# Polysketch attention and a sigmoid-gated FFN in one kernel: a denominator's sum moved forward on ScalarE, a product batch moved ahead of the Gram sums, and one PSUM bank exchanged

## The chip, the core and the metric

The kernel runs on one core of a Trainium2 chip. The metric is the device time of an execution in microseconds (us). It was 308.38 us in the median of six runs of the kernel before (308.05 to 309.17).

The engines have short names in the profile: PE is TensorE (matrix products), PEld is its loading of weights, DVE is VectorE, ACT is ScalarE, POOL is GpSimd, SP is SyncE, which here only issues DMAs. Each engine works through its own list of instructions in the order in which the program gives them. Between engines semaphores make one wait for another.

## What is computed

```python
# q, k, v: (4, 4, 1088, 32) = batch, heads, tokens, head_dim; S1, S2: (8, 32)
def phi(x):
    a = einsum('rd,bhsd->bhsr', S1, x)
    b = einsum('rd,bhsd->bhsr', S2, x)
    return einsum('bhsi,bhsj->bhsij', a, b).reshape(..., 64)
q_p, k_p = phi(q), phi(k)
kv  = einsum('bhsf,bhsd->bhfd', k_p, v)
z   = sum(k_p, axis=2)
num = einsum('bhsf,bhfd->bhsd', q_p, kv)
den = einsum('bhsf,bhf->bhs', q_p, z)[..., None] + 1e-06
x   = (num / den), laid out as (4352, 128) = (batch * tokens, heads * head_dim)
# w_gate, w_val: (128, 1536), w_out: (1536, 128)
out = (1 / (1 + exp(-(x @ w_gate))) * (x @ w_val)) @ w_out
```

The three weights and S1, S2 arrive as 64-bit numbers and are narrowed to 32 bits on the chip.

## The kernel before

**The FFN.** The 4352 tokens are cut into chunks of 512 (`tok_chk`), the 1536 hidden columns into 12 blocks of 128. `w1` makes a *wave*: for one chunk and one block, the gate and value products (L350) into a PSUM tile `wave`, and the sigmoid of the first on ScalarE (`sg`, L358). `glu` multiplies the two on VectorE (`g`, L371). `w2` multiplies by the block of w_out and adds up over the blocks in PSUM (`moeout`, L307), two waves behind. `slot(group, n)` emits a group of attention work and then n waves, so most of the attention of batches 1 to 3 lies between waves. In the first chunk the first wave is split into halves of 256 columns. The tokens of that chunk come from batch 0, so batch 0's first half of q must go through the attention before any wave can begin. That stretch, from the start to the first waves, is called the head here. All the edits lie in it.

**Order.** The program puts PE, DVE, ACT and POOL under a schedule written by hand (`tc.manual_schedule`): the order of calls in the code is the order of instructions on these four engines. Waits between engines, and waits for a tile's buffer to come free, are put in by the framework from what each instruction reads and writes.

**The head's attention, in the order of the code.** `turn_k` and `turn_q` transpose k and q in 32x32 blocks. `kps(0)` multiplies k by the sketches into PSUM tile `two`, and VectorE transposes that into `kab` (two instructions, L448). `ab((0, 0, 0))` and `ab((0, 1, 0))` make the a-products of q for the two pairs of heads (PSUM `wave`; ScalarE copies them to `asb`). `gram()` makes 36 small products of kab with itself (L460), from which z is formed; its PSUM tile is in bank `acc1`. ScalarE copies the result (`gs`), GpSimd masks it (`gh`). `spread_z` multiplies again (L487). `mask_z` puts the result into `zb` on VectorE (L498, L510). `ab(None, ...)` makes the b-products of q: those of pair 0 in tile `two`, those of pair 1 in a `wave` tile. It returns `mult00` or `mult10`, which multiply a and b on VectorE into `qp` (L567). `outer` (L520) forms the features of k, first for blocks 0 to 4, later for 5 to 8, and `kv0` (L628) adds their products with v up in `kvz`, bank `acc0`.

**`dn` and `divide`.** `dn(b, n, mid)` makes the denominators `dps` (L720; for batch 0's first half in bank `acc1`), then calls `mid`, then makes the numerators `nps` (L733). For the head `mid` is `rest`: the remaining `outer` and `kv0`, `kvd` (ScalarE copies kvz, L664), `ndt` (TensorE transposes the copy into bank `acc0`, L698, and ScalarE copies that to `nd`, L711). `dn` returns `divide`. This transposes dps (`dT`), adds 1e-6 (`rc`), takes the reciprocal (L752), spreads it with a transposition (`rb`, L756) and multiplies (`xT`, L767). In the head the sum with 1e-6 is on ScalarE (`sum_on_act`). In all other calls it is on VectorE (L751). `warm` gives TensorE a product that nobody reads.

**Narrowing.** `narrow` is a generator in four steps: step 0 clamps the high words on GpSimd (`cap`, L97) and scales the low words on ScalarE (`tail`, L101). Step 1 shifts and joins bits on VectorE (`head`, L105 and L109). Step 2 squares cap on ScalarE (`square`, L117, in a PSUM bank) and adds head and tail on GpSimd (L118). Step 3 combines the square and the sum on VectorE into `w_sb` (L121). `narrow_01(part, step)` does the first two columns' weights in three parts: part 0 is gate and value of column 0, part 1 those of column 1, part 2 the w_out of both. `narrow_w(j, step)` does column j, and `w1` calls it for columns 2 and up between the waves of the first chunk. The squares lie in PSUM banks `acc0` and `acc1`, each with one buffer, which the sums `moeout` use too. A new tile in a bank waits until the last reader of the tile before is through.

The weights' DMAs (`load_w`, six groups of three) are issued on SP from the start, after k, the sketches, the first half of q, and v.

Of the kernel before, what the change touches and what calls it, by code (L numbers as in the profile page):

```python
# [8 lines left out]
F32 = mybir.dt.float32  # L9
# [4 lines left out]
ACTF = mybir.ActivationFunctionType  # L14
MUL = ALU.mult

P = 128
# [3 lines left out]
def kernel(  # L21
# [12 lines left out]
    nc = tc.nc  # L34
# [19 lines left out]
    sbA = ctx.enter_context(tc.tile_pool(name="sbA", bufs=2))  # L54
# [124 lines left out]
    def narrow_01(part, step):  # L179
        if wide:  # L180
            if step == 0:
                i = (slice(0, 2), part) if part < 2 else (2, slice(0, 2))
                narrowing["01", part] = narrow(
                    w_sb[:, i[0], i[1]],
                    w_in[0][:, i[0], i[1]],
                    nc.gpsimd,
                    "acc0" if part == 1 else "acc1",
                )
            next(narrowing["01", part])

# [54 lines left out]
    def warm(*cols):  # L245
        t = psm.tile([P, 2, 512], F32, tag="wave", name="warm")
        one = [bass.AP(tensor=ones.tensor, offset=ones.offset, ap=[list(ones.ap[0]), [0, n]]) for n in cols]
        x = bass.AP(tensor=ones.tensor, offset=ones.offset, ap=[list(ones.ap[0]), [0, P]])
        for r in one:
            n = r.shape[-1]  # L250
            nc.tensor.matmul(out=t[:, 0, :n], lhsT=x, rhs=r, start=True, stop=True)  # L251
# [18 lines left out]
    for c in range(2):  # L270
        rows = slice(64 * c, 64 * c + 64)
        nc.vector.tensor_reduce(
            out=m_col[rows, c],
            in_=ident[rows].rearrange("p (k j) -> p j k", j=R),
# [3 lines left out]
    for t, x in ((e_row, id_h.rearrange("p h x -> p x h")), (e_head, id_h)):  # L278
        nc.vector.tensor_reduce(out=t, in_=x, axis=mybir.AxisListType.X, op=ALU.add)
    nc.vector.tensor_copy(  # L280
        out=e_sum,
# [6 lines left out]
    eps = const.tile([P, 1], F32, tag="eps")  # L288
    nc.gpsimd.memset(eps, 1e-6)
    zb = []  # L290
    for n in range(2):
        t = const.tile([P, H, 32], F32, tag=f"zb{n}", name=f"zb{n}")
# [239 lines left out]
    def ab(a_of=None, b_of=None, pool_b=None):  # L532

        mm = []
        if a_of is not None:
            aps = psm.tile([P, 2, 512], F32, tag="wave", name="aps")
            mm.append((a_of, aps, sa))
        if b_of is not None:
            pool, tag = (ps2, "two") if pool_b is None else pool_b
            bps = pool.tile([P, 2, 512], F32, tag=tag, name="bps")  # L540
            mm.append((b_of, bps, sb))
        for c in range(2):
            for m in range(2):
                for (bb, pr, n), dst, sx in mm:
                    h = 2 * pr + m
                    rows = slice(32 * h, 32 * h + 32)
                    t0, tn = q_chk[n]
                    nc.tensor.matmul(
                        out=dst[64 * c : 64 * c + 64, m, : 32 * tn],
                        lhsT=sx[rows, :],  # L550
                        rhs=qT_of[bb][rows, t0 : t0 + tn, c, :],
                        start=True,
                        stop=True,
                    )
        if a_of is not None:
            w = 32 * q_chk[a_of[2]][1]
            ASB[a_of] = sbA.tile([P, 2, 256], F32, tag="asb", name="asb", bufs=2)
            nc.scalar.copy(out=ASB[a_of][:, :, :w], in_=aps[:, :, :w])
        if b_of is not None:

            def mult():
                bb, pr, n = b_of
                if bb not in QP:
                    QP[bb] = sbA.tile([P, 2 * H * W1], F32, tag="qp", name="qp")
                t0, tn = q_chk[n]
                w = 32 * tn
                nc.vector.tensor_tensor(  # L567
                    out=half(QP[bb], n).rearrange("p (m c) w -> p c m w", m=2)[:, pr],
                    in0=bps[:, :, :w],
                    in1=ASB[b_of][:, :, :w],  # L570
                    op=MUL,
                )

            return mult
# [47 lines left out]
    def kv0(j_list):  # L622
        if 0 not in KVZ:
            KVZ[0] = pso.tile([P, TCH], F32, tag="acc0", name="kvz")
        for j in j_list:
            kr = 64 if j == 0 else P
            for h in range(H):
                nc.tensor.matmul(  # L628
                    out=KVZ[0][32 * h : 32 * h + 32, :F],
                    lhsT=v_t[0][:kr, h, j, :],  # L630
                    rhs=KP[0][:kr, h // 2, j, h % 2, :],
                    start=(j == 1),
                    stop=(j == NJK - 1),
                    skip_group_check=True,
                )
# [24 lines left out]
    def kvd(b):  # L660
        KVD[b] = sbA.tile([P, 2, 2, F], F32, tag="kvd", name="kvd")
        k0 = KVZ[b][:, : 2 * F]
        n = 2 if b > 0 else 1
        nc.scalar.copy(  # L664
            out=KVD[b][:, :n],
            in_=bass.AP(
                tensor=k0.tensor, offset=k0.offset, ap=[list(k0.ap[0]), [F, n], [0, 2], [1, F]]
            ),
        )
# [44 lines left out]
    def dn(b, n, mid=None):  # L714
        t0, tn = q_chk[n]
        w = 32 * tn
        bank = (moe["sum"] + 1) % 2 if moe["sum"] >= 0 else 1
        dps = pso.tile([P, TCH], F32, tag=f"acc{bank}", name="dps")
        for h in range(H):
            nc.tensor.matmul(  # L720
                out=dps[32 * h : 32 * h + 32, :w],
                lhsT=zb[b % 2][:, h, :],
                rhs=half(QP[b], n)[:, 2 * (h % 2) + h // 2, :],
                start=True,
                stop=True,
            )
        if mid is not None:
            mid()
        t = ps2.tile([P, 2, 512], F32, tag="two", name="nps")
        for h in range(H):  # L730
            for c in range(2):
                rows = slice(64 * c, 64 * c + 64)
                nc.tensor.matmul(  # L733
                    out=t[32 * h : 32 * h + 32, c, :w],
                    lhsT=ND[b][rows, 32 * h : 32 * h + 32],
                    rhs=half(QP[b], n)[rows, 2 * (h % 2) + h // 2, :],
                    start=True,
                    stop=True,
                )

        def divide(*parts, between=None, sum_on_act=None):
            dT = sbA.tile([P, 9, 32], F32, tag="dT", name="dT")
            nc.vector.transpose(out=dT[:, :tn].rearrange("p t c -> p (t c)"), in_=dps[:, :w])
            rc = sbA.tile([P, 9, 2], F32, tag="rc", name="rc")
            if sum_on_act is not None:
                nc.scalar.activation(
                    out=rc[:, :tn], in_=dT[:, :tn, :2], func=ACTF.Identity, bias=eps
                )
                sum_on_act()
            else:  # L750
                nc.vector.tensor_scalar_add(rc[:, :tn], dT[:, :tn, :2], 1e-6)  # L751
            nc.vector.reciprocal(out=rc[:, :tn], in_=rc[:, :tn])  # L752
            rb = sbA.tile([P, 9, 2, 32], F32, tag="rb", name="rb")
            for u0, u1 in parts or [(0, tn)]:
                r0 = rc[:, u0:u1]
                nc.vector.transpose(  # L756
                    out=rb[:, u0:u1].rearrange("p t c s -> p (t c s)"),
                    in_=bass.AP(
                        tensor=r0.tensor,
                        offset=r0.offset,  # L760
                        ap=[list(r0.ap[0]), [1, 2 * (u1 - u0)], [0, 32]],
                    ),
                )
                if between is not None and u0 == 0:
                    between()
                o = b * S + 64 * (t0 + u0)
                nc.vector.tensor_tensor(  # L767
                    out=xT[:, o : o + 64 * (u1 - u0)].rearrange("p (t c s) -> p c t s", c=2, s=32),
                    in0=t[:, :, 32 * u0 : 32 * u1].rearrange("p c (t s) -> p c t s", s=32),
                    in1=rb[:, u0:u1].rearrange("p t c s -> p c t s"),  # L770
                    op=MUL,
                )
            moe["ready"] = b * S + 64 * (t0 + tn)

        return divide

    steps = narrow(sr, sr_in, nc.vector) if wide else iter(())
    for _ in range(3):
# [9 lines left out]
        out=sk,  # L788
# [21 lines left out]
    kps(0)  # L810
    ab((0, 0, 0))
    ab((0, 1, 0))
    spread_z, mask_z = gram()
    mult00 = ab(None, (0, 0, 0))
    mult10 = ab(None, (0, 1, 0), (psm, "wave"))
    for part in range(3):
        narrow_01(part, 0)
# [6 lines left out]
    mask_z()  # L824


    def rest():
        for pi in range(2):
            outer(0, pi, 5, NJK)
        kv0(range(5, NJK))  # L830
        kvd(0)
        ndt(0)

    divide = dn(0, 0, rest)
    warm(512)

    def head0():
        narrow_01(0, 1)
        narrow_01(0, 2)

    def head1():
        narrow_01(1, 1)
# [2 lines left out]
        narrow_w(2, 0)  # L845
        narrow_w(3, 0)

    divide((0, 4), (4, 8), between=head1, sum_on_act=head0)
    narrow_01(1, 3)
    narrow_01(2, 1)  # L850
    narrow_01(2, 2)
# [85 lines left out]
```

## Time and profile before

One execution was profiled. It took 309.17 us, the highest of the six. Its span, from the first to the last instruction, is 307.3 us; 1.87 us lie around it.

| what | value |
|---|---|
| median of six runs | 308.38 us (308.05 to 309.17) |
| profiled execution: time, span | 309.17 us, 307.3 us |
| TensorE's granted clock | 1.000 |
| PE busy, 0 to 7.40 us | 4.71 us |
| PE busy, 7.40 to 23.50 us | 13.24 us of 16.10 |
| PE busy, 23.50 to 303.40 us | 279.65 us of 279.90 |
| DMA, 7.40 to 23.50 us | 341 GB/s |
| DVE, ACT, POOL busy, 7.40 to 23.50 us | 13.86, 7.34, 7.15 us |

A row of the timeline gives the start, the busy time, the engine, the line of the code, the operation, the tile written and those read, the shape, and a count: neighbouring instructions of one kind are put together. The bracket at its end is the time for which the engine sat idle before it, and what ended the wait. Where a wait is for several things, the bracket names the one that the profile saw last, which need not be the one that mattered. Rows of one engine can overlap by about 0.1 us[...]. The waits view adds up who waited for whom. The chain of waits goes back from the last instruction, each time to what released it.

### The profile page before, as it was taken

How to read it: one execution, taken by the hardware profiler on the slowest of the kernel's cores; microseconds unless marked ns; L12 is line 12 of the kernel's file. 1: busy time of each engine (PE TensorE's matmuls, PEld its weight loads, DVE VectorE, ACT ScalarE, POOL GpSimd, SP SyncE). 2: the span in 40 equal slices, each digit the busy share in tenths (PEclk: the TensorE clock that was granted, in tenths of full speed). 3: DMA queues.
4: the chain of work that ended last, by engine and by line, in shares of the span. 5: the costliest groups of instructions: out<-in, count | busy, mean ns of one | idle time of the engine just before them, and what ended most of it. 6: DMA issues, size and time to landing. Idle time of an engine off the chain costs nothing.

```text
span 307.3 us, 3606 instructions
## 1 busy us (share of the span) xinstructions
PE 297.6 (97%) x1361; PEld 136.4 (44%) x1361; DVE 155.0 (50%) x268; ACT 80.4 (26%) x150; POOL 34.8 (11%) x63
## 2 busy tenths in 40 slices
PE   6889999999999999999999999999999999999994
PEld 2433434444344444543444444444444444444683
DVE  4978789752836544463565542645232223222331
ACT  3355542322122222222123222212222222222220
POOL 2165541230000320000002300000000000000000
PEclk9999999999999999999999999999999999999999
DMA  7991422399602292242003920200001000200011
GB/s 205 360 335 45 122 63 114 80 174 169 185 0 34 71 221 56 60 104 96 0 0 87 235 61 2 35 0 2 0 10 24 0 0 5 31 0 0 6 29 17
DMA packets 29842, 23.35 MB, mean 76 GB/s; under 512 B 21185, under 2 KB 24769, under 8 KB 29825
## 3 DMA queue, kind: packets, MB, share of 16 engines
q1 hardware_dynamic: 25456, 15.28, 18.7%
q0 software_dynamic: 3456, 7.09, 11.6%
q10 hardware_dynamic: 912, 0.77, 1.0%
q8 instruction: 10, 0.16, 0.2%
q14 instruction: 8, 0.06, 0.1%
HBM read 19.86 MB, written 3.26 MB: 75 GB/s over the span
## 4 chain that ended last, share of the span: by engine, by line
PE 84%; DMA 10%; DVE 2%; POOL 1%; SPq 1%; issue 0%; ACT 0%; DVEq 0%; POOLq 0%
PE wave L350 52%; PE moeout L307 27%; DMA bq<-dq 4%; DMA w_in<-in_moe_w_val_dram 2%; DMA w_in<-in_moe_w_gate_dram 2%; DMA v<-in_v_dram 1%; PE nps L733 1%; PE dps L720 1%; PE kvz L642 1%; DMA out_dram<-o_sb 1%; PE cqps L587 1%; PE kps L438 1%; POOL qp L611 1%; POOL bq L611 0%; DVE head L109 0%; SPq L328 0%
## 5 line engine op out<-in xcount | busy, mean ns | idle before, releaser
L350 PE MATMUL wave<-xT,w_sb 128*128 128x512 f32 (+1 forms) x436 | 191.8, 565 | 0.6 <-DVE xT L767 0.6
L371 DVE TENSOR_TENSOR g<-wave,sg 128x512 f32<-128x512 f32 x102 | 70.4, 690 | 128.3 <-ACT sg L358 128.0
L350 PEld LDWEIGHTS wave<-xT,w_sb 128*128 128x128 f32 x436 | 82.6, 190 | 94.7 <-issue 87.0
L358 ACT ACTIVATE sg<-wave 128x512 f32<-128x512 f32 x102 | 61.0, 598 | 202.6 <-PE wave L350 202.6
L307 PE MATMUL moeout<-g,w_sb 128*128 128x512 f32 (+1 forms) x216 | 105.5, 576 | 0.6 <-DVE w_sb L121 0.4
L307 PEld LDWEIGHTS moeout<-g,w_sb 128*128 128x128 f32 x216 | 39.4, 190 | 44.6 <-issue 37.8
L611 POOL DMA_DIRECT2D qp<-dq x12 | 7.0, 587 | 110.3 <-DMA dq<-cq 110.3
L118 POOL TENSOR_TENSOR head<-head,tail 128x384 int32<-128x384 int32 (+2 forms) x14 | 13.4, 959 | 21.2 <-DVE head L109 13.6
L620 DVE TENSOR_TENSOR qp<-qp,bq 128x1152 f32<-128x1152 f32 (+1 forms) x7 | 9.1, 1295 | 4.6 <-DMA bq<-dq 4.6
L520 DVE TENSOR_TENSOR kp<-kab 128x1152 f32<-128x1152 f32 (+2 forms) x10 | 10.8, 1096 | 0.0
L109 DVE SCALAR_TENSOR_TENSOR head<-cap,head 128x384 int32<-128x384 int32 (+2 forms) x14 | 7.5, 538 | 0.5
L121 DVE SCALAR_TENSOR_TENSOR w_sb<-square,head 128x384 f32<-128x384 f32 (+1 forms) x11 | 5.7, 519 | 3.9 <-POOL head L118 3.2
L317 DVE STREAM_TRANSPOSE o_sb<-moeout 128x512 f32<-128x512 f32 (+1 forms) x9 | 6.1, 680 | 2.6 <-PE moeout L307 2.5
L611 POOL DMA_DIRECT2D bq<-dq x12 | 6.9, 576 | 0.5 <-DMA out_dram<-o_sb 0.2
L97 POOL TENSOR_SCALAR cap<-w_in 128x384 f32<-128x384 f32 (+1 forms) x13 | 6.8, 532 | 0.0
L251 PE MATMUL warm<-ones 128*128 128x512 f32 x8 | 5.8, 874 | 1.0 <-DVE hm L257 1.0
L101 ACT ACTIVATE tail<-w_in 128x384 int32<-128x384 uint32 (+1 forms) x13 | 6.5, 519 | 0.0
L767 DVE TENSOR_TENSOR xT<-nps,rb 128x576 f32<-128x576 f32 (+2 forms) x9 | 5.9, 660 | 0.7
L756 DVE STREAM_TRANSPOSE rb<-rc 128x576 f32<-128x576 f32 (+2 forms) x9 | 6.1, 681 | 0.3
L720 PE MATMUL dps<-qp,zb 128*32 128x256 f32 (+1 forms) x64 | 5.3, 404 | 0.7 <-DVE zb L510 0.7
L733 PE MATMUL nps<-qp,nd 64*32 64x256 f32 (+1 forms) x128 | 5.5, 401 | 0.4 <-ACT nd L711 0.4
L426 DVE STREAM_TRANSPOSE qT<-kq 128x512 f32<-128x512 f32 (+1 forms) x8 | 5.7, 714 | 0.0
(72 smaller groups left out, 83.6 us busy)
## 6 DMA issues: line engine op xcount, KB each, us to landing
qp<-dq POOLq DMA_DIRECT2D x12, 288.0 KB, 7.7
bq<-dq POOLq DMA_DIRECT2D x12, 288.0 KB, 8.4
v<-in_v_dram SPq DMA_DIRECT2D x16, 144.0 KB, 5.2
kq<-in_k_dram SPq DMA_DIRECT2D x3, 544.0 KB, 3.8
kq<-in_q_dram SPq DMA_DIRECT2D x3, 544.0 KB, 4.9
w_in<-in_moe_w_gate_dram SPq DMA_DIRECT2D x6, 256.0 KB, 5.3
w_in<-in_moe_w_val_dram SPq DMA_DIRECT2D x6, 256.0 KB, 6.1
w_in<-in_moe_w_out_dram SPq DMA_DIRECT2D x6, 256.0 KB, 6.9
```

Of the source, the lines that this page charges most:

```text
L97: eng.tensor_scalar(out=cap.bitcast(F32), in0=hi.bitcast(F32), scalar1=122880.0, scalar2=-122880.0, op0=ALU.min, op1=ALU.max,)
L109: nc.vector.scalar_tensor_tensor(out=head, in0=cap, scalar=-0x40000000, in1=head, op0=ALU.bitwise_and, op1=ALU.bitwise_or)
L118: nc.gpsimd.tensor_tensor(out=head, in0=head, in1=tail, op=ALU.add)
L307: nc.tensor.matmul(out=moe["acc"][:, :tw], lhsT=w_sb[:, 2, j, :], rhs=g[:, jj, :tw], start=(j == 0), stop=(j == NJ - 1),)
L350: nc.tensor.matmul(out=wv[:, which, jj * tw + o : jj * tw + o + tp], lhsT=w_sb[:, which, j0 + jj, :], rhs=xT[:, t0 + o : t0 + o + tp], sta ...
L358: nc.scalar.activation(out=sg, in_=wv[:, 0], func=ACTF.Sigmoid)
L371: nc.vector.tensor_tensor(out=g, in0=wv[:, 1], in1=sg, op=MUL)
L520: nc.vector.tensor_tensor(out=KP[b][:, pi, j0:j1].rearrange("p j m (i l) -> p (j m) i l", i=R), in0=bass.AP(tensor=a0.tensor, offset=a0.of ...
L611: get.dma_start(out=t[64 * c : 64 * c + 64, n * H * W1 : (n + 1) * H * W1], in_=bass.AP(tensor=d0.tensor, offset=d0.offset, ap=rows + [[1, ...
L620: nc.vector.tensor_tensor(out=q0, in0=q0, in1=half(BQ[b], n), op=MUL)
L720: nc.tensor.matmul(out=dps[32 * h : 32 * h + 32, :w], lhsT=zb[b % 2][:, h, :], rhs=half(QP[b], n)[:, 2 * (h % 2) + h // 2, :], start=True, ...
L733: nc.tensor.matmul(out=t[32 * h : 32 * h + 32, c, :w], lhsT=ND[b][rows, 32 * h : 32 * h + 32], rhs=half(QP[b], n)[rows, 2 * (h % 2) + h // ...
```

## The change

There are four edits, all in the head.

1. `mult00 = ab(None, (0, 0, 0))`, the b-products of pair 0, is called before `gram()` and not after it.
2. `dT` and `rc` are made in `dn`, and `rest` now transposes dps (`turn`) right after the second part of `kv0` and puts the sum with 1e-6 on ScalarE at once, ahead of `kvd`'s copy. The steps 1 and 2 of part 0's narrowing, which `divide` called after the sum, now come between `kvd` and `ndt`. `divide` in the head begins with the reciprocal.
3. The square of part 2 goes to bank `acc0`, where part 1's is, and no longer to `acc1`.
4. `warm` after the numerators has 256 columns for 512.

```diff
@@ narrow_01
-                    "acc0" if part == 1 else "acc1",
+                    "acc0" if part else "acc1",
...
@@ dn
+        dT = sbA.tile([P, 9, 32], F32, tag="dT", name="dT")
+        rc = sbA.tile([P, 9, 2], F32, tag="rc", name="rc")
+
+        def turn():
+            nc.vector.transpose(out=dT[:, :tn].rearrange("p t c -> p (t c)"), in_=dps[:, :w])
+
         if mid is not None:
-            mid()
+            mid(turn, rc, dT)
...
-        def divide(*parts, between=None, sum_on_act=None):
-            dT = sbA.tile([P, 9, 32], F32, tag="dT", name="dT")
-            nc.vector.transpose(out=dT[:, :tn].rearrange("p t c -> p (t c)"), in_=dps[:, :w])
-            rc = sbA.tile([P, 9, 2], F32, tag="rc", name="rc")
-            if sum_on_act is not None:
-                nc.scalar.activation(
-                    out=rc[:, :tn], in_=dT[:, :tn, :2], func=ACTF.Identity, bias=eps
-                )
-                sum_on_act()
-            else:
+        def divide(*parts, between=None):
+            if mid is None:
+                turn()
                 nc.vector.tensor_scalar_add(rc[:, :tn], dT[:, :tn, :2], 1e-6)
             nc.vector.reciprocal(out=rc[:, :tn], in_=rc[:, :tn])
...
     ab((0, 1, 0))
+    mult00 = ab(None, (0, 0, 0))
     spread_z, mask_z = gram()
-    mult00 = ab(None, (0, 0, 0))
     mult10 = ab(None, (0, 1, 0), (psm, "wave"))
...
-    def rest():
+    def rest(turn, rc, dT):
         for pi in range(2):
             outer(0, pi, 5, NJK)
         kv0(range(5, NJK))
+        turn()
+        nt = rc.shape[1] - 1
+        nc.scalar.activation(out=rc[:, :nt], in_=dT[:, :nt, :2], func=ACTF.Identity, bias=eps)
         kvd(0)
-        ndt(0)
-
-    divide = dn(0, 0, rest)
-    warm(512)
-
-    def head0():
         narrow_01(0, 1)
         narrow_01(0, 2)
+        ndt(0)
+
+    divide = dn(0, 0, rest)
+    warm(256)
...
-    divide((0, 4), (4, 8), between=head1, sum_on_act=head0)
+    divide((0, 4), (4, 8), between=head1)
```

More of the change, by code (lines that the diff above doesn't have):

```diff
@@ L830, in rest @@
         kv0(range(5, NJK))
+        turn()
+        nt = rc.shape[1] - 1
+        nc.scalar.activation(out=rc[:, :nt], in_=dT[:, :nt, :2], func=ACTF.Identity, bias=eps)
         kvd(0)
+        narrow_01(0, 1)
+        narrow_01(0, 2)
         ndt(0)
     divide = dn(0, 0, rest)
-    warm(512)
-    def head0():
-        narrow_01(0, 1)
-        narrow_01(0, 2)
+    warm(256)
     def head1():
```

## The prediction

> **What bounds the kernel now.** I read the page's busy shares first, then the stretches, then each engine's timeline from 8 to 33 us, then the waits.
>
> ```profile
> PE 297.6 (97%) x1361; PEld 136.4 (44%) x1361; DVE 155.0 (50%) x268; ACT 80.4 (26%) x150; POOL 34.8 (11%) x63
> ```
>
> By stretches TensorE is busy 279.65 of 279.90 us between 23.50 and 303.40, but only 13.24 of 16.10 us between 7.40 and 23.50. Its one later gap, 0.25 us at 79.10, ends a chain that TensorE itself starts. So the kernel ends earlier by what the wave at 23.50 gains. PE's timeline shows the last waits ahead of it:
>
> ```profile
> 16.56 1.13 PE L251 MATMUL warm<-ones 128*128 128x512 f32 x2
> 18.24 3.71 PE L350 MATMUL wave<-xT,w_sb 128*128 128x256 f32 x12 [0.55 <-DVE xT L767]
> 22.31 1.12 PE L307 MATMUL moeout<-g,w_sb 128*128 128x512 f32 x2 [0.36 <-DVE w_sb L121]
> 23.50 1.98 PE L350 MATMUL wave<-xT,w_sb 128*128 128x512 f32 x4
> ```
>
> Two VectorE results stand there: xT, then narrowed weights. VectorE (second column: busy time; bracket: idle time before):
>
> ```profile
> 11.35 1.29 DVE L567 TENSOR_TENSOR qp<-bps,asb 128x512 f32<-128x512 f32 x2 [0.21 <-PE bps L548]
> ...
> 14.79 0.42 DVE L109 SCALAR_TENSOR_TENSOR head<-cap,head 128x256 int32<-128x256 int32 x1
> 16.15 0.25 DVE L752 RECIPROCAL rc<-rc 128x16 f32<-128x16 f32 x1 [0.94 <-ACT rc L746]
> 16.44 0.45 DVE L756 STREAM_TRANSPOSE rb<-rc 128x256 f32<-128x256 f32 x1
> 16.81 0.25 DVE L105 TENSOR_SCALAR head<-cap 128x256 int32<-128x256 int32 x1
> ...
> 19.25 0.30 DVE L105 TENSOR_SCALAR head<-cap 128x256 int32<-128x256 int32 x1
> ...
> 20.31 1.01 DVE L109 SCALAR_TENSOR_TENSOR head<-cap,head 128x384 int32<-128x384 int32 x1
> ...
> 22.89 0.56 DVE L121 SCALAR_TENSOR_TENSOR w_sb<-square,head 128x384 f32<-128x384 f32 x1 [0.63 <-ACT square L117]
> ```
>
> Between 7.4 and 23.5 it idles in just three places worth a tenth of a us: 0.21, 0.94 and 0.63. The change has an edit for each. ScalarE and GpSimd:
>
> ```profile
> 15.65 0.27 ACT L711 COPY nd<-ndps 128x128 f32<-128x128 f32 x1 [0.42 <-PE ndps L698]
> 15.81 0.31 ACT L746 ACTIVATE rc<-dT,eps 128x16 f32<-128x16 f32 x1
> ...
> 22.29 0.49 ACT L117 ACTIVATE square<-cap 128x384 f32<-128x384 f32 x1 [0.97 <-DVE w_sb L121]
> ```
> ```profile
> 15.36 0.72 POOL L118 TENSOR_TENSOR head<-head,tail 128x256 int32<-128x256 int32 x1 [2.94 <-ACT kvd L664]
> 17.67 0.72 POOL L118 TENSOR_TENSOR head<-head,tail 128x256 int32<-128x256 int32 x1 [1.58 <-DMA w_in<-in_moe_w_gate_dram]
> ...
> 20.87 0.84 POOL L97 TENSOR_SCALAR cap<-w_in 128x384 f32<-128x384 f32 x1
> 21.68 0.99 POOL L118 TENSOR_TENSOR head<-head,tail 128x384 int32<-128x384 int32 x1
> ```
>
> On ScalarE the sum comes behind both copies, and w2's square waits for a VectorE reader; on GpSimd the additions of part 0, part 1 and w2 each follow an L109, the last behind a cap. Parts 0, 1, 2 are the first narrowed tiles (gate and value of column 0, of column 1, both w_out); w2 is the next column.
>
> **Edit 1, b-products first.** No instruction is added. The eight products need kps' PSUM tile free, after the second kab transposition (8.84 and 0.85: 9.69), so they start at 9.74 instead of 10.55. Both batches took 0.69 together; one alone is over by 10.45. VectorE finishes its outer products at 9.61 + 1.52 = 11.13 and can start the multiplication 0.08 before that, as its rows overlap: 11.05 for 11.35, **-0.30**. The Gram products move back: those after the second transposition took 9.74 to 10.61, 0.87; started at 10.0 they end near 10.8, 0.15 to 0.2 later. Behind them wait gs' copy and three tails on ScalarE, gh and three caps on GpSimd (to 12.42, now 12.6, first read at 14.20), and the other b-products (over by 11.4, wanted at 11.65). The sums' second product and kvz move from 12.52 to 12.7; dps is wanted at 12.87. Covers are 0.2 us or more. Bounds: 0 (a cover fails) to -0.31; I take -0.30, since the idle time and the overlap are both measured.
>
> **Edit 2, denominator early.** The transposition of dps stays first on VectorE after the second outer products (14.14, now 13.84). Its sum runs at once on ScalarE, at 14.35 for 0.31. It is now ahead of kv's copy, which queues behind it; the copy, which began at 14.96, has its input at 14.66 and a ScalarE row lets the next begin about 0.1 before its end (nd ends 15.92, rc begins 15.81), so at 14.56: no cost, 0.1 cover. If lost, what follows is the path copy, ndps, nd, nps, xT. Part 0's square also slips ahead of nd: 0.38 or less from 14.95, done by 15.35, nd wanted at 15.35 to 15.45: nothing. nps, whose row is 15.97 and 0.67, is ready at 16.34 for 16.64.
> VectorE narrows part 0 at 14.49 (L109) and takes the reciprocal 0.34 later (the step from L109 at 17.10 to L121 at 17.44): 14.83 for 16.15, **-1.32** with edit 1 in it.
>
> **What comes late next: the port.** Part 0's addition on GpSimd starts 0.15 after L109 ends (15.21 to 15.36): now 15.06 to 15.78. Until now VectorE sat idle through it. Now part 1's L105 falls due at 15.49. Durations without neighbours (0.25 at 16.81) give no loss. The Trainium skill, "SBUF — State Buffer", section "SBUF: two separate sides", speaks against it: VectorE and GpSimd share a port pair as an exclusive lock when VectorE runs a two-port mode or reads two SBUF inputs, and the loser blocks for the whole instruction. The trace agrees: L109 of w2 took 1.01 (0.56 at 23.74) with GpSimd's addition beside it from 20.18 for 0.73, and ended 0.41 after it; L105 at 19.25 took 0.30 for 0.25, blocked till a cap ended at 19.40. By the rule L105 waits until 15.78 and ends near 15.95 for 15.74: **+0.20**; by the plain rows 0. I take the rule's. At worst the whole addition blocks, +0.5.
>
> From there VectorE runs the same order without idle time: reciprocal, rb, L105, L109, L121, xT, second half, part 1, part 2, w2. Each moves by -1.12: xT from 17.77 to 16.65 (nps ready, 0.3 cover), the first wave from 18.24 to 17.12, part 2's L109 from 19.58 to 18.46. The caps of w2 and w3 again run beside that L105, and GpSimd's chain to w2's addition (20.18 to 22.67, back to back) starts from that L109: its end goes to 21.55.
>
> **Edit 3, bank.** w2's square waited (22.29, idle 0.97) until L121 at 21.84 had read part 2's square in the same bank. Now it waits for part 0's reader, near 16.7, and runs after the first sigmoid and tail: about 20.1 to 20.6, 0.95 under the addition. L121 of w2 then hangs on the addition alone: 21.6 for 22.89. That is **-1.29**; the bank gives 0.17 of it. The new wait: part 2's square behind L121 of part 1, 18.2; it ends near 18.6, with the first sigmoid queued behind it (due 19.15) and its reader at 20.7. Nothing. moeout's first product needs that same reader anyway.
>
> **Edit 4, warm-up.** With 512 columns it would end at 17.69 - 0.30 = 17.39 and hold the wave due at 17.12. With 256 it ends near 16.85. Nothing, and it must be halved.
>
> **Behind 23.50.** Weights and TensorE both start from L121 of w2, so they keep their distance. It matters: the last L121 ends 49.01 and its wave begins 49.06, no slack.
>
> **Sum:** -0.30 - 1.02 + 0.20 - 0.17 = **-1.29 us**. The profiled execution took 309.17 (span 307.3 and 1.87 around it): 307.88. It is the highest of the six; against the median of 308.38 I predict **307.1**. About 0.2% (0.62 us) is what such runs can tell from no change.
>
> **Rivals.** *Half the gain*: edit 1 fails to show (the other b-products or Gram sums late) or the port costs its worst: -0.99, **307.4**. For it: covers of 0.1 to 0.2; against: durations are steady.
> *The weights' DMA bounds it.* The bracket at 17.67 names a landing, and the chain of waits goes through it. Then part 1's addition stays at 17.67, its L121 moves only to 18.4, and the gain is 0.5 + 0.17: 307.7; if w4's cap stays at 20.87 too, only 0.17 is left: **308.2**. Against: part 1's addition starts 0.15 after its L109 (17.10 + 0.42), the same lag as part 0's, whose weights were long there, and w_in takes 5.2 to 6.9 us to land, so w4's, issued by 10.2, is there by 17.1.
> *Slower: the clock gate.* The Trainium skill, "TensorE: Matmul & The Clock Gate", section "What's actually happening", has the array at half rate until about 3.4 us of sustained work, and again after such an idle window. The trace shows the cold pace at the start (weight loads of warm at 1.98, 2.83, 3.68: 0.85 apart, 0.43 later). If half as much warm-up lets the gate close, each 3.4 us window costs 1.7: one gives 307.1 + 1.7 = 308.8, two **310.5**; it decides from one window on. Against: the granted clock is 1.00 in all stretches and gaps get shorter, 0.65 at most.
>
> **Numbers.** Forecast 62%, half 20%, DMA 11% (a third of it near 307.7), clock 7%. Faster: 62 + 20 + 3 = 85%; same: 8 of the DMA case and 1 of the clock, 9%; slower 6%. The range 306.7 to 307.8 holds the first two and that third, with 0.4 below for a collision at 20.31 that dissolves.
>
> **What would show it.** Reciprocal near 14.8 with no idle time; L105 near 15.5 stretched to 0.45; xT near 16.65; w2's square near 20.1 and its L121 released by GpSimd at 21.6; the wave at 22.2, then no new gap. A reciprocal beyond 15.2, kv's copy beyond 14.75 or a first wave in passes of 0.43 for 0.22 would make it wrong.

## The result and the profile after

The changed kernel takes **0.9965** of the time of the kernel before (95% interval 0.995 to 0.998): faster by 0.35%, or about 1.1 us, where 1.29 were predicted. Its median is 307.99 us over 35 runs, just above the predicted range (306.7 to 307.8). But the median of the kernel before, over 72 runs, is 309.12 and not the 308.38 of the six runs first shown. The lowest times of the two kernels, 307.83 and 306.91, lie 0.92 apart. The medians are of all runs; the ratio leaves out executions more than 1.5% above the fastest of their kernel. The profiled execution took 307.84 us with a span of 305.7.

TensorE's timeline after:

```profile
9.51 0.66 PE L548 MATMUL bps<-qT,s 32*64 32x256 f32 x8 [0.37 <-DVE kab L448]
10.10 0.88 PE L460 MATMUL gram<-kab 64*32 64x32 f32 x36
10.91 0.66 PE L548 MATMUL bps<-qT,s 32*64 32x256 f32 x8
...
16.33 0.70 PE L251 MATMUL warm<-ones 128*128 128x256 f32 x2
17.18 3.71 PE L350 MATMUL wave<-xT,w_sb 128*128 128x256 f32 x12 [0.16 <-DVE xT L766]
21.25 1.12 PE L307 MATMUL moeout<-g,w_sb 128*128 128x512 f32 x2 [0.35 <-DVE w_sb L121]
22.27 1.98 PE L350 MATMUL wave<-xT,w_sb 128*128 128x512 f32 x4
```

The wave of column 2 begins at 22.27 for 23.50. Not all of that is the change's. VectorE's first kab transposition, ahead of everything that was edited, began at 8.52 for 8.84; the row before, then after:

```profile
8.84 0.85 DVE L448 STREAM_TRANSPOSE kab<-kps 128x288 f32<-128x288 f32 x2 [0.22 <-PE kps L438]
```
```profile
8.52 0.85 DVE L448 STREAM_TRANSPOSE kab<-kps 128x288 f32<-128x288 f32 x2 [0.22 <-PE kps L438]
```

From here on times are counted from that start, the anchor, since it moved between 8.08 and 8.84 from one profiled execution to another; where a time is given "on the old axis", 0.32 is added to a time of the trace after. So counted, the wave moved from 14.66 to 13.76: **0.90 us** (the rounded starts above give 13.75 and 0.91). VectorE after:

```profile
10.72 0.68 DVE L567 TENSOR_TENSOR qp<-bps,asb 128x512 f32<-128x512 f32 x1
11.71 0.69 DVE L567 TENSOR_TENSOR qp<-bps,asb 128x512 f32<-128x512 f32 x1 [0.30 <-PE bps L548]
...
14.56 0.43 DVE L109 SCALAR_TENSOR_TENSOR head<-cap,head 128x256 int32<-128x256 int32 x1
14.90 0.25 DVE L751 RECIPROCAL rc<-rc 128x16 f32<-128x16 f32 x1
15.18 0.45 DVE L755 STREAM_TRANSPOSE rb<-rc 128x256 f32<-128x256 f32 x1
15.55 0.46 DVE L105 TENSOR_SCALAR head<-cap 128x256 int32<-128x256 int32 x1
...
18.19 0.30 DVE L105 TENSOR_SCALAR head<-cap 128x256 int32<-128x256 int32 x1
...
19.26 1.01 DVE L109 SCALAR_TENSOR_TENSOR head<-cap,head 128x384 int32<-128x384 int32 x1
...
21.66 0.56 DVE L121 SCALAR_TENSOR_TENSOR w_sb<-square,head 128x384 f32<-128x384 f32 x1 [0.46 <-POOL head L118]
```

The idle 0.94 ahead of the reciprocal is gone. So is the 0.21 ahead of the first multiplication, but 0.30 now stands ahead of the second. (The 0.22 ahead of kab stands in both kernels: before, VectorE had four idle places, not the three that the prediction counts, but this one lies ahead of the edits.) L105 of part 1 is stretched from 0.25 to 0.46. Column 2's last step is released by GpSimd's addition, no longer by the square. ScalarE and GpSimd:

```profile
14.44 0.31 ACT L832 ACTIVATE rc<-dT,eps 128x16 f32<-128x16 f32 x1 [2.25 <-DVE dT L731]
14.73 0.27 ACT L664 COPY kvd<-kvz 128x128 f32<-128x128 f32 x1
...
20.15 0.51 ACT L117 ACTIVATE square<-cap 128x384 f32<-128x384 f32 x1
```
```profile
15.13 0.72 POOL L118 TENSOR_TENSOR head<-head,tail 128x256 int32<-128x256 int32 x1 [2.44 <-ACT kvd L664]
16.61 0.73 POOL L118 TENSOR_TENSOR head<-head,tail 128x256 int32<-128x256 int32 x1 [0.75 <-DVE head L109]
...
20.63 1.00 POOL L118 TENSOR_TENSOR head<-head,tail 128x384 int32<-128x384 int32 x1
```

The addition of part 0 (15.13 to 15.85) lies beside the stretched L105 (15.55 to 16.01). That of part 1 is now released by VectorE's L109, earlier than the landing that the bracket before had named.

### The profile page after: what moved, and what is told of

It is laid out like the page before. It is cut to its first block, busy times and chain, and to the rows that moved or that the text cites. A ratio compares the mean times of both kernels' runs of the same rounds, so it can differ in the third digit from the quotient of the medians.

```text
span 305.7 us, 3606 instructions
## 1 busy us (share of the span) xinstructions
PE 297.0 (97%) x1361; PEld 136.3 (45%) x1361; DVE 155.1 (51%) x268; ACT 80.7 (26%) x150; POOL 34.8 (11%) x63
## 4 chain that ended last, share of the span: by engine, by line
PE 93%; DVE 4%; DMA 1%; issue 0%; POOL 0%; SPq 0%; POOLq 0%; DVEq 0%
PE wave L350 56%; PE moeout L307 30%; PE nps L739 1%; PE dps L720 1%; PE kvz L642 1%; DMA sr_in<-in_S_dram 1%; PE kps L438 1%; DVE head L109 1%; PE cqps L587 1%; DVE head L105 0%; PE bps L548 0%; DVE kp L520 0%; DVE kab L448 0%; DVE w_sb L121 0%; PE gram L460 0%
## 5 line engine op out<-in xcount | busy, mean ns | idle before, releaser
L520 DVE TENSOR_TENSOR kp<-kab 128x1152 f32<-128x1152 f32 (+2 forms) x10 | 10.8, 1096 | 0.0
L109 DVE SCALAR_TENSOR_TENSOR head<-cap,head 128x384 int32<-128x384 int32 (+2 forms) x14 | 7.5, 538 | 0.5
L121 DVE SCALAR_TENSOR_TENSOR w_sb<-square,head 128x384 f32<-128x384 f32 (+1 forms) x11 | 5.7, 518 | 3.8 <-POOL head L118 3.8
L251 PE MATMUL warm<-ones 128*128 128x512 f32 (+1 forms) x8 | 5.0, 764 | 1.0 <-DVE hm L257 1.0
L117 ACT ACTIVATE square<-cap 128x384 f32<-128x384 f32 (+1 forms) x11 | 5.1, 461 | 1.6 <-DVE w_sb L121 1.5
```

The costliest lines, as they stand in the source:

```text
L109: nc.vector.scalar_tensor_tensor(out=head, in0=cap, scalar=-0x40000000, in1=head, op0=ALU.bitwise_and, op1=ALU.bitwise_or)
L520: nc.vector.tensor_tensor(out=KP[b][:, pi, j0:j1].rearrange("p j m (i l) -> p (j m) i l", i=R), in0=bass.AP(tensor=a0.tensor, offset=a0.of ...
```

## The experiments

The places on the path, in us from the anchor; "rec." is the reciprocal, "L105" the length of part 1's, "last" the start of column 2's L121, "wave" the first product of column 2's wave. "Half clock" is where in the head a stretch of 3.41 us at half TensorE clock begins. Each row is one execution.

| profiled execution | 1st, 2nd mult. | rec. | L105 | xT | first wave | last | wave | half clock |
|---|---|---|---|---|---|---|---|---|
| before | 2.50, 3.11 | 7.31 | 0.25 | 8.93 | 9.40 | 14.04 | 14.66 | none |
| after | 2.21, 3.19 | 6.38 | 0.46 | 8.20 | 8.67 | 13.14 | 13.76 | none |
| e1 Gram first | 2.50, 3.11 | 6.29 | 0.46 | 8.34 | 9.18 | 13.31 | 14.26 | 6.74 |
| e2 sum late | 2.21, 3.19 | 7.40 | 0.25 | 9.02 | 9.49 | 13.95 | 14.56 | none |
| e3 bank back | 2.21, 3.19 | 6.38 | 0.46 | 8.19 | 8.66 | 13.31 | 13.92 | none |
| e4 no addition | 2.21, 3.19 | 6.37 | 0.25 | 7.99 | 8.46 | 12.93 | 13.55 | none |
| e5 warm 512 | 2.21, 3.19 | 6.38 | 0.46 | 8.20 | 8.78 | 13.14 | 13.75 | none |
| e6 no warm-up | 2.21, 3.19 | 6.38 | 0.46 | 8.20 | 8.67 | 13.72 | 14.82 | 9.05 |
| e7 both b first | 2.21, 2.81 | 6.51 | 0.46 | 8.33 | 8.80 | 13.27 | 13.88 | none |
| e8 filled | 2.21, 3.47 | 6.38 | 0.46 | 8.20 | 8.67 | 13.15 | 13.76 | none |
| e9 after, late mult. | 2.21, 3.19 | 6.38 | 0.46 | 8.20 | 8.67 | 13.15 | 13.77 | none |
| e10 before, late mult. | 2.50, 3.11 | 7.31 | 0.25 | 8.93 | 10.03 | 14.48 | 15.09 | 7.08 |
| e11 late, Gram first | 2.50, 3.11 | 6.29 | 0.46 | 8.11 | 8.58 | 13.05 | 13.66 | none |
| e12 late, no warm-up | 2.21, 3.19 | 6.38 | 0.46 | 8.20 | 8.67 | 13.95 | 15.05 | 8.69 |

**e1: edit 1 undone.**

```diff
-    mult00 = ab(None, (0, 0, 0))
     spread_z, mask_z = gram()
+    mult00 = ab(None, (0, 0, 0))
```

> The changed kernel with edit 1 alone undone: the Gram products come first again, the other three edits stay. Times are counted from the start of the first kab transposition (before 8.84, after 8.52), since what lies ahead of it shifts from one execution to the next. Theory A: edit 1 gave nothing, because the Gram products now hold up the b-products of pair 1 and VectorE waits ahead of its second multiplication instead of its first. Then VectorE idles about 0.2 us ahead of the first multiplication, the wave of column 2 begins 13.65 to 13.85 us after the anchor, as in the changed kernel (13.75), and the time is the changed kernel's. Theory B, the prediction's: edit 1 is worth 0.30 us. Then the wave begins near 14.05, and the ratio to the kernel before is about 0.001 nearer to 1 than the changed kernel's.

Measured: ratio 0.9959 (0.9939 to 0.9979), no slower than with the edit. The reciprocal comes 0.09 us earlier without it. That is theory A as far as the reciprocal. But the wave came at 14.26, outside both expectations, and the trace shows why: the clock. By stretches (the figure after the comma is TensorE's busy time, the third from the end the granted clock):

```profile
11.63:15.04 3.41, 2.10 (x57) 1.10 (x49) 3.31 (x10) 1.02 (x4) 0.56 (x2) 1.00 1.08 378
15.04:18.45 3.41, 3.06 (x22) 1.81 (x22) 3.15 (x10) 1.79 (x5) 2.20 (x4) 0.50 1.05 371
```

For 3.41 us TensorE had half its clock; nps took 1.11 us for 0.67 and the waves came late. e11, below, has the same head and met no such stretch. Its VectorE (anchor at 8.32):

```profile
10.82 1.29 DVE L567 TENSOR_TENSOR qp<-bps,asb 128x512 f32<-128x512 f32 x2 [0.21 <-ACT tail L101]
...
14.61 0.24 DVE L751 RECIPROCAL rc<-rc 128x16 f32<-128x16 f32 x1
```

**e2: edit 2 left out.** The kernel before with edits 1 and 3:

```diff
-    spread_z, mask_z = gram()
     mult00 = ab(None, (0, 0, 0))
+    spread_z, mask_z = gram()
...
-                    "acc0" if part == 1 else "acc1",
+                    "acc0" if part else "acc1",
```

> The kernel before with edits 1 and 3 alone: edit 2 is left out (transposition, sum and reciprocal in the old order, 512 warm columns). Theory A: edit 2 carries the gain; VectorE idles about 0.9 us ahead of the reciprocal again, the wave of column 2 begins 14.4 to 14.65 us after the first kab transposition (before 14.66, after 13.75), and the time is within 0.1% of the kernel before. Theory B: the gain came from elsewhere (weights or sketches that landed earlier in that execution); then the wave begins near 13.75 and the time stays near 0.9965.

Measured: wave at 14.56, theory A. The ratio is 1.0018 (0.999 to 1.0047), a little above the 0.1% that A allowed, with an interval that holds it. The profile has the old wait back, and edit 1 makes it no earlier: 7.40 for 7.31.

```profile
15.48 0.25 DVE L752 RECIPROCAL rc<-rc 128x16 f32<-128x16 f32 x1 [0.94 <-ACT rc L746]
```

**e3: the bank put back.**

```diff
-                    "acc0" if part else "acc1",
+                    "acc0" if part == 1 else "acc1",
```

> The changed kernel with edit 3 alone undone: part 2's square is in bank acc1 again. Theory A: w2's square waits for part 2's reader, begins right behind it, and w2's last VectorE step begins about 0.16 us later; the wave of column 2 at 13.85 to 13.95 us after the first kab transposition (13.75 in the changed kernel). Theory B: GpSimd's addition sets w2 in either case and the bank is worth nothing: 13.75.

Measured: wave 13.92, 0.16 us later than in the changed kernel, theory A; ratio 0.9973 (0.9951 to 0.9994). VectorE and ScalarE of this kernel:

```profile
21.42 0.56 DVE L121 SCALAR_TENSOR_TENSOR w_sb<-square,head 128x384 f32<-128x384 f32 x1 [0.63 <-ACT square L117]
```
```profile
20.82 0.49 ACT L117 ACTIVATE square<-cap 128x384 f32<-128x384 f32 x1 [0.98 <-DVE w_sb L121]
```

**e4: no addition for part 0.** This kernel leaves out the low words of column 0's gate and value weights.

```diff
-    def narrow(out, bits, eng, bank=None):
+    def narrow(out, bits, eng, bank=None, skip=False):
...
-        nc.gpsimd.tensor_tensor(out=head, in0=head, in1=tail, op=ALU.add)
+        if not skip:
+            nc.gpsimd.tensor_tensor(out=head, in0=head, in1=tail, op=ALU.add)
...
                     "acc0" if part else "acc1",
+                    part == 0,
```

> The changed kernel without GpSimd's addition of head and tail for part 0, so the low words of column 0's gate and value are left out. Theory A, the port: VectorE's first step for part 1, 0.46 us in the changed kernel, takes 0.25 again because GpSimd is idle beside it, and everything behind it on VectorE, xT included, comes 0.2 us earlier (xT 8.0 us after the first kab transposition for 8.20, the wave of column 2 at 13.55). Theory B: the step is long because it waits for its own input or for the transposition ahead of it; then it stays at 0.46 and nothing moves.

Measured, on VectorE:

```profile
15.47 0.25 DVE L105 TENSOR_SCALAR head<-cap 128x256 int32<-128x256 int32 x1
```

0.25 again, xT at 7.99 and the wave at 13.55, each 0.21 earlier: theory A. L105 begins 7.02 us after the anchor here (at 8.45) and 7.03 in the changed kernel: there it was stretched and not late, so it did not wait for an input. The one time taken is 311.92, for a reason outside the head. In this execution a DMA of batch 1's spread landed late. A q multiplication waited 6.35 us for it, and the gated products queue behind that multiplication (line numbers are two higher in this kernel):

```profile
78.57 1.36 DVE L622 TENSOR_TENSOR qp<-qp,bq 128x1152 f32<-128x1152 f32 x1 [6.35 <-DMA bq<-dq]
79.84 0.68 DVE L373 TENSOR_TENSOR g<-wave,sg 128x512 f32<-128x512 f32 x1
```
```profile
80.58 2.07 PE L309 MATMUL moeout<-g,w_sb 128*128 128x512 f32 x2 [3.25 <-DVE g L373]
```

TensorE stood for 3.25 us and came back in a stretch of 3.41 us at half clock, so that this product took 2.07 for 1.12. The gap goes with the multiplication's wait: 0.18 us of gap for a wait of 3.53 in e2, 0.25 for 3.60 before, 0.49 for 3.84 in e3, 1.16 for 4.53 in e7, 3.25 for 6.35 here, and none where the wait was 3.23 or less (after, e1, e5, e6, e8).

**e5 and e6: the warm-up.**

```diff
-    warm(256)
+    warm(512)
```
```diff
-    warm(256)
```

> The changed kernel with 512 warm columns for 256. Theory A, the prediction's step: the warm-up now lies in front of the first wave and holds it by 0.1 to 0.3 us (it began 8.66 us after the first kab transposition). But the wave of column 2 hangs on VectorE and GpSimd, and the first gated product has 0.35 us to spare behind VectorE's long step, so it stays at 13.75. Theory B: the first wave is on the path, and the wave of column 2 moves by as much as the first.

> The changed kernel without the warm-up ahead of the first wave; no output depends on it. Theory A: TensorE's clock is full long before, the first waves take 0.22 us for 256 columns as before, and nothing moves (wave of column 2 at 13.75 us after the first kab transposition). Theory B, the clock gate: without it the array falls back to half pace for a window, the first two waves take up to 3.7 us longer in sum, and the time is up to 0.5% longer than the changed kernel's.

With 512 columns (one execution, 307.94) the first wave moved by 0.11 us and column 2's by nothing: theory A. Without the warm-up (0.9989, 0.9962 to 1.0015) the clock halved right ahead of the first waves, and they took 5.40 us for 3.71:

```profile
16.98 5.40 PE L350 MATMUL wave<-xT,w_sb 128*128 128x256 f32 x12 [0.78 <-DVE xT L766]
```

That is theory B in the trace; how often it happens is told below, after e12. The stretches of e6, and below them those of the changed kernel, whose clock windows lay at the same distance from the anchor (boundary at 5.63 there, 5.65 here):

```profile
13.95:17.36 3.41, 1.91 (x47) 1.05 (x47) 3.27 (x11) 2.42 (x7) 1.67 (x3) 1.00 1.07 373
17.36:20.78 3.42, 3.42 (x9) 2.58 (x8) 2.62 (x6) 0.70 (x2) 2.63 (x5) 0.50 1.06 373
```
```profile
14.17:17.58 3.41, 2.53 (x49) 1.34 (x46) 3.27 (x11) 2.42 (x7) 1.70 (x3) 1.00 1.07 371
```

With 1.91 us of TensorE work in a window the next one is at half clock, with 2.53 it is not. The difference is the warm-up, whose row is 0.70.

**e7 and e8: where the 0.30 us went.**

```diff
-    spread_z, mask_z = gram()
     mult10 = ab(None, (0, 1, 0), (psm, "wave"))
+    spread_z, mask_z = gram()
```
```diff
     mult00()
+    outer(0, 0, 5, NJK)
     mult10()
...
-        for pi in range(2):
-            outer(0, pi, 5, NJK)
+        outer(0, 1, 5, NJK)
```

> The changed kernel with the b-products of both pairs ahead of the Gram products. Theory A: VectorE's two multiplications follow each other without idle time, but the Gram sums come 0.3 us later and VectorE now waits for them ahead of the masking (zm): the wait only moves on, and xT stays within 0.1 us of 8.20 us after the first kab transposition. Theory B: the Gram chain has cover enough; then the 0.30 us of edit 1 appear in full, xT at 7.9, the wave of column 2 at 13.45.

> The changed kernel with one of the two later outer products put between VectorE's two multiplications, where it idles 0.30 us. Theory A: the idle time is filled, and what is late next is dps, so that 0.1 to 0.2 us are won: xT 8.0 to 8.1 us after the first kab transposition (8.20), the wave of column 2 near 13.6. Theory B: dps and the port take all of it back: 8.20 and 13.75.

VectorE of e7, then of e8:

```profile
10.67 1.28 DVE L567 TENSOR_TENSOR qp<-bps,asb 128x512 f32<-128x512 f32 x2
12.25 0.22 DVE L498 TENSOR_TENSOR zm<-gram,m_col 128x64 f32<-128x64 f32 x1 [0.30 <-PE gram L487]
```
```profile
13.79 0.45 DVE L731 STREAM_TRANSPOSE dT<-dps 128x256 f32<-128x256 f32 x1 [0.23 <-PE dps L720]
```

In e7 the multiplications follow each other at last, and the 0.30 us stand ahead of the Gram sums' mask instead; the reciprocal is 0.13 later, and so is xT, a little more than theory A allowed. In e8 the gap is filled with an outer product. The second multiplication then ends later, TensorE waits 0.39 us for zb behind it before it can make dps, and VectorE, which has one outer product less to do meanwhile, waits 0.23 for dps. xT stays at 8.20: theory B. The times agree: e7's one execution took 308.80 (with a gap of 1.16 us near 79), e8's ratio (0.9969, 0.9949 to 0.9988) is the changed kernel's.

**e9 to e12: without batch 1's wait.** To judge the head with less scatter, the multiplication that waits for the last spread was put behind the next group, for batch 1 alone:

```diff
-        qmult(b, 1)
-        load_kq(b + 1)
+        if b > 1:
+            qmult(b, 1)
+            load_kq(b + 1)
         slot(lambda: part(b, 0), wn)
+        if b == 1:
+            qmult(b, 1)
+            load_kq(b + 1)
```

This went into the changed kernel (e9), the kernel before (e10), the changed one with the Gram products first (e11, the edit of e1) and without warm-up (e12, the edit of e6).

> The changed kernel, with one thing more: for batch 1 VectorE's second q multiplication, which waits for the last spread DMA, and the next load of k and q are emitted after the first half's division group, so that the gated products no longer queue behind that wait. So far this wait has stopped TensorE near 77 to 80 us for 0 to 3.2 us, another amount in each profiled execution, whatever the edit. Theory A: it makes the scatter; without it there is no TensorE gap after the head, the time is 306.7 to 307.3 us and the ratio to the kernel before 0.993 to 0.996, with a narrower spread than the changed kernel's. Theory B: the wait only moves to the next group (the second half's division, or the next k); then a gap of like size stands a few us later and the ratio stays at 0.9965.

> The kernel before with the same late multiplication for batch 1, so that the four edits can be judged without the stall. Theory A: the head's edits are worth 0.9 us (wave of column 2 at 14.66 us after the first kab transposition for 13.75), so this kernel takes 0.8 to 1.0 us longer than the changed kernel with the late multiplication (e9). Theory B, the prediction's: 1.29 us.

> e9's kernel with edit 1 undone. Theory A: edit 1 is worth nothing in time where the clock is full (first reciprocal 6.29 us after the first kab transposition for 6.38), so the fastest executions equal e9's within 0.15 us. Where a half-clock window of 3.41 us falls into the head, as in the first look at the Gram products first, the wave of column 2 comes 0.5 us later. Theory B, the prediction's: 0.30 us slower than e9 in the fastest executions too.

> e9's kernel without the warm-up ahead of the first wave. Theory A, the clock gate: in the executions whose clock windows fall so that the idle time ahead of the first wave counts, the array works a window of 3.41 us at half clock, the wave of column 2 comes about 1 us later, and the median is 0.3 to 1.0 us above e9's, with fastest executions that equal e9's. Theory B: the half clock seen in the first look was chance and has nothing to do with the warm-up; then the median is e9's.

| run | median, lowest to highest (runs) | ratio to before |
|---|---|---|
| e9 | 307.44, 306.89 to 308.22 (10) | 0.9970 (0.9959 to 0.9980) |
| e10 | 308.45, 307.88 to 310.71 (14) | 1.0002 (0.9981 to 1.0022) |
| e11 | 307.47, 306.89 to 307.88 (5) | 0.9968 (0.9955 to 0.9981) |
| e12 | 307.71, 306.88 to 308.29 (11) | 0.9972 (0.9959 to 0.9984) |

None of the four traces has a TensorE gap after the head, and e9's ten times lie within 1.4 us where the changed kernel's 35 went from 306.91 to 314.25. But the ratio stays near 0.997 and missed the expected 0.993 to 0.996: the wait feeds the long times and not the typical one. e10 less e9 is 1.01 us in the median and 0.99 in the lowest time, nearer to theory A's 0.9 than to the predicted 1.29; e10's profiled execution had a half-clock stretch besides (wave at 15.09). e11 equals e9 (lowest 306.89 in both), and its trace puts the wave at 13.66: edit 1 costs 0.09 us where the clock is full. e12's median is 0.27 above e9's, short of what theory A expected, and its lowest time is the same; its trace again has the half clock, and the wave at 15.05.

**How often the clock halves.** Every execution's mean granted clock is on record, not only the profiled ones'. It is either 0.997 and more or 0.994 and less; one stretch of 3.41 us at half clock in a span of 306 us makes 0.994. It does not tell where the stretch lay.

| run | executions at 0.994 or less | their median | median of the others |
|---|---|---|---|
| e9 and e11 | 0 of 15 | | 307.47 |
| e12, no warm-up | 4 of 11 | 308.06 | 307.15 |
| e10, kernel before | 5 of 14 | 309.20 | 308.32 |

So without the warm-up, and in the kernel before, some executions meet the half clock and take about 0.9 us longer; with the warm-up and edit 2 none of 15 did. That is theory A of e12, though its median came out lower than A said, since seven of the eleven met none. Of the kernels with batch 1's wait, e6 has 8 of 15 and the changed one 7 of 36 (the profiled execution counted), where the stretch can also lie behind that wait, as in e4. With the executions at half clock left out, e10 less e9 is 0.88 us: the head's 0.90.

## Why the prediction was right and wrong

**The bound was right.** From column 2's wave to its last product TensorE took 279.91 us before and 279.56 after, the stall near 79 being 0.25 of the difference. The head gained 0.90 us, the lowest times differ by 0.92, and the ratio, 1.1 us, has an interval of 0.6 to 1.5.

**Step by step**, the head's sum against what one change at a time showed:

| term | predicted | measured | by |
|---|---|---|---|
| edit 1, b-products first | -0.30 | +0.09 | reciprocal 6.38 for 6.29 (e11, e1) |
| edit 2, denominator early | -1.02 | -1.02 | 6.29 for 7.31 (e11 against before) |
| "the port", part 1's L105 | +0.20 | +0.21 | xT 8.20 for 7.99 (e4) |
| edit 3, bank | -0.17 | -0.16 | wave 13.76 for 13.92 (e3) |
| sum | -1.29 | -0.88 | wave 13.76 for 14.66: -0.90 |

**The step that failed in the head is edit 1's covers.** The prediction let the Gram products start 0.26 us after the b-products (10.0 for 9.74) and be over near 10.8. In the old rows the two batches of b-products ran side by side, 16 products in 0.69 us:

```profile
9.39 1.22 PE L460 MATMUL gram<-kab 64*32 64x32 f32 x36
10.55 0.69 PE L548 MATMUL bps<-qT,s 32*64 32x256 f32 x16
```

Edit 1 parts them, and each alone takes 0.66. Nor do they run beside the Gram products, which have another shape: before, the b-products began 0.06 before the Gram row's end, and after, the Gram products began 0.07 before the end of the first batch's row. So the Gram products started 0.59 after the first batch (9.51 to 10.10) and took 0.88. The second batch ended at 11.57, which is 11.89 on the old axis, and not at 11.4; VectorE wanted it at 11.65, and its second multiplication waited 0.30. The prediction named that cover, "0.2 us or more", and its failure as the lower bound, 0. It was slightly below: +0.09. In e7 and e8 two other orders gained nothing either: VectorE's wait moved on to the Gram sums or to dps. The rival "half the gain" (-0.99) was nearest in the head (measured -0.90), for the reason that it gave first: the other b-products were late.

**The step that failed outside is the base.** The predicted time was the median of six runs less the sum, and the range had no term for the executions' own scatter. This is what put the time outside the range: the measured ratio times 308.38 is 307.3, and even 308.38 less the head's 0.90 is 307.48, both within it. But the kernel before itself, beside these runs, had 309.12. In the three later series its median was 308.40, 308.63 and 308.31, near the six runs. Its lowest time hardly moved (307.83 here, 307.74 to 307.90 there). What moved is the share of executions more than 1.5 us above the lowest: 33 of 72 here, 16 of 51, 8 of 38 and 2 of 28 there. Why that share was so high beside this result stays open; batch 1's wait and the half clock feed it. Some of the scatter lies outside the span: in six of the changed kernel's 36 executions time and span differ by 2.3 to 3.3 us, where the median is 1.8. The sentence that the later gap "ends a chain that TensorE itself starts" was true of its start and wrong as a constant: the gap was 0 to 3.25 us in the profiled executions and went with the wait for a DMA's landing.

**Luck in the signs.** In raw times nearly all that the prediction said would show it came: reciprocal 14.90, L105 at 15.55, xT 16.72, the square 20.15, its L121 21.66, the wave 22.27. That is because this execution's head began 0.32 us earlier. On the old axis they are 15.22, 15.87, 17.04, 20.47, 21.98 and 22.59, each about 0.4 late, and two of the signs of being wrong appeared: a reciprocal beyond 15.2, and kv's copy, at 15.05, beyond 14.75.

**Right:** the sum on ScalarE ran ahead of kv's copy at no cost. The copy began 0.29 after the sum, at 14.73, when its product's row ended at 14.68; before, the same two were 14.96 and 14.92. Part 2's square, which now waits in the other bank, ended at 18.70, and the first sigmoid's input came at 19.22. That the warm-up must be halved was too strong: at 512 columns the first wave comes 0.11 us later (e5), and the path does not feel it.

**Rivals.** The weights' DMA did not bound the head: GpSimd's addition of part 1 moved with VectorE's L109 (16.61 after). The bracket that named a landing was the last of several waits and not the one that counted. The clock gate did not make the change slower, but it deserved more than 7%, and it worked the other way: it was the kernel before that met the half clock more often (e10 against e9 and e11). Among the profiled executions a half-clock stretch in the head came in one of two with the Gram products first, in one of three without edit 2, and in both without the warm-up; in none of the other seven (after, e3, e4, e5, e7, e8, e9).

## What to carry to other kernels

A step that is moved ahead on a busy engine delays what it passes, so its cover is to be computed from the moved work's own duration alone, not from a row in which it overlapped with something else. A gain of a third of a percent is judged by times from a common anchor in the traces, one edit at a time, and by the lowest times; the median of the same kernel moved by 0.8 us between two series of runs. And earlier work can land beside another engine's instruction and be stretched by it, as L105 was: count that collision before counting the gain.

## What the runs showed of the hardware

**The clock halved without an idle window.** Half clock came in windows of 3.41 us. In the head it followed windows in which TensorE's rows were busy for 2.10 (e1), 1.91 (e6), 1.79 (e10) and 1.66 us (e12), with no gap in them over 0.8 us. The window of the changed kernel (2.53) and those of the kernel before (2.38 and 2.22, one after the other) were not followed by it. The windows of e10, e12 and the second of the kernel before:

```profile
11.78:15.19 3.41, 1.79 (x42) 0.95 (x41) 2.64 (x8) 0.54 (x3) 0.59 (x2) 1.00 1.08 377
```
```profile
13.59:17.00 3.41, 1.66 (x46) 0.82 (x46) 3.31 (x11) 2.41 (x7) 1.32 (x2) 1.00 1.06 371
```
```profile
15.00:18.41 3.41, 2.22 (x20) 0.79 (x21) 2.40 (x8) 2.58 (x8) 1.47 (x3) 1.00 1.05 373
```

The Trainium skill, "TensorE: Matmul & The Clock Gate", section "What's actually happening", names a window of about 3.4 us, which agrees, and a fall after at least one idle window; by that none of these four would have fallen. Busy time is not the whole measure either: the first window at full clock of the kernel before and of the changed one, with the first long wait in it, had 1.5 to 1.6 us and was followed by full clock. What else counts stays open. Since the windows lie otherwise against the program in each execution, the same head can meet the half clock (e1) or not (e11). It put column 2's wave off by 0.4 to 1.3 us here.

**VectorE's L105 was held until GpSimd's addition was over.** Due at 15.55, L105 of part 1 ended 0.16 us after the addition beside it ended at 15.85, and took 0.46 for 0.25; without the addition (e4) it took 0.25. At w2's L109 the same 1.01 us for 0.56 stood before and after, since both sides moved together: the addition there began 0.13 before it in either kernel.
